# Look-ahead of five pairs in place of eight, inverses in groups of two on two engines, and a later M product, in a chunked scan with two MLPs

## The chip, the cores and the metric

One NeuronCore of a Trainium2 chip runs one launch. Times are microseconds of device time; the span in a profile is the time from the first to the last instruction of one profiled execution. Engines are named as in the profile: PE is TensorE (PEld its weight loads), DVE VectorE, ACT ScalarE, POOL GpSimd, SP SyncE, which only issues DMAs here.

## The reference

For each of 4 x 8 heads a state of 40 x 40 is carried over 768 steps, then two MLPs follow:

```python
for t in range(S):                                   # B, H, S, D = 4, 8, 768, 40
    y[:, :, t] = np.einsum('bhd,bhde->bhe', rt, state)
    Sa = np.einsum('bhde,bhe->bhd', state, at)
    state_decay = state * wt[:, :, None, :] - np.einsum('bhd,bhe->bhde', Sa, bt)
    state = state_decay + np.einsum('bhd,bhe->bhde', vt, kt)
x = y.transpose(0, 2, 1, 3).reshape(3072, 320)
xn = x / rms(x) * rms_g                              # first MLP, d_ff 1536
x = (silu(xn @ w_gate) * (xn @ w_val)) @ w_out
h = x @ w_in                                         # second MLP, d_ff 2048
out = (h - np.tanh(h)) @ w_out2
```

## The kernel before

**Scan.** Time is cut into 12 chunks of 64 steps. A *unit* is one chunk of one batch entry with its eight heads; a *pair* is the same chunk of two entries, so there are 48 units and NP = 24 pairs, and one pass of the main loop, a *period*, deals with one pair. Inside a chunk the recurrence is a triangular system. What it needs is prepared ahead of the loop's current pair, by LOOKP pairs:

- `load_p`, `emit_p` (lines 201 to 231): load a unit, two scans over its decays on VectorE (lines 218 and 222, with a reciprocal at 221), three products on GpSimd (228 to 230). `spill_p` (234) writes the result to HBM, `load_q`, `load_kl` and `load_e` bring the parts back when the pair's turn has come. The first units keep their results in SBUF (`fp`, the pool `first`), later ones use the tile `arena`.
- `emit_m` (236): the product of a pair's units on TensorE (line 247, 32 matmuls), copied by ScalarE and written to HBM as `md` (line 252), by SP's queue where the pool `fp` is used and by ScalarE's queue otherwise.
- `inverse` (254): for a group of pairs (`GROUPS`), the diagonal blocks of M are read back (line 270) and inverted by 31 steps of two instructions on the engine `eng` (lines 276 and 278); the result goes to HBM as `td` (282) and comes back as TT (`load_t`, 347). Group 0 runs on VectorE, all others on GpSimd; groups 0 and 1 have two pairs, the later ones four.

**A period's chain** on TensorE: right side (`emit_rhs`, 397), solve with TT (`emit_u`, 408), product with MX (`emit_w`, 417; VectorE subtracts at 418), solve again (`emit_u2`, 425; `emit_ut`, 472), state (`emit_d`, 437; VectorE at 442 to 448), `emit_z` (482; VectorE 484), `emit_mak` (384; VectorE 387) and `emit_s` (462) for the next pair, `emit_e` (372). The next period finishes the output (`emit_y`, 505 and 507) and normalizes it (`emit_x1`: GpSimd at 514 and 515, VectorE's scaling at 516).

**MLPs.** Between the steps `moe` puts pieces of the first MLP into TensorE's order: an up half (`up`, line 554, 8 matmuls) or a down set (559 to 561, 6 matmuls). It has 12 blocks of 256 tokens with 12 steps of two up halves and one down set each. VectorE joins the halves (576, 578), ScalarE and GpSimd split the result in two (581, 582). Where a call of `moe` finds no piece it issues 8 filler matmuls (`warm`, 288). Until the second block begins, `piece` lets only M_PER pieces through per period, from period M_FIRST on:

```python
if begun[0] < 2 and period[0] < M_FIRST + pieces[0] // M_PER:
    return 0.0
```

The weights come as 64-bit words; a *weight task* (`split_words`, 136 to 151) is one load, ScalarE's absolute value (140), five instructions on VectorE (141 to 146), ScalarE's copy (147) and two instructions on GpSimd (150, 151). The first MLP has 48 tasks: 16 go to tiles that are free from the start, 32 to the pool `w1p`, whose memory is that of `first`. The second MLP's tasks are started by `some2` in the last periods, and go on behind the loop; the last three of its eight chunks use the first MLP's memory.

**Order.** TensorE's instructions stand as the code is written. For the other engines a scheduler sorts them by the priorities that `when`, `later` and `step` set; in the prologue their order is written out too. Each engine then works off its queue in order. `issue_after` only tells the scheduler what must stand ahead.

## Time and profile before

| | us |
|---|---|
| median of 3 runs (lowest, highest) | 1404.84 (1403.24, 1406.26) |
| profiled execution: device time | 1405.97 |
| profiled execution: span | 1403.9 |
| mean granted TensorE clock | 0.937 |

| engine | busy us | share of the span |
|---|---|---|
| PE | 1230.0 | 88% |
| DVE | 689.3 | 49% |
| ACT | 465.2 | 33% |
| POOL | 738.5 | 53% |

First product of a period (line 397), start in us: period 0 at 36.3, 1 at 123.7, 2 at 165.6, 3 at 196.2, 4 at 232.3, 5 at 272.9, 6 at 310.4, 7 at 349.1, 8 at 378.4, 9 at 429.8, 15 at 653.5, 23 at 933.6. The second MLP's first matmul starts at 1032.1. The page's slices are a fortieth of the span each (35.1 us), and a digit is the busy share in tenths. In a table of windows each row gives the stretch, its length, each engine's busy time and number of instructions, the granted clock, the DMA engines' share and GB/s. A row of waits gives the instruction that waited, what released it, the total us, the times, and the longest.

### The profile page before, as it was taken

The numbers are of one execution on the slowest core, as the hardware profiler recorded it, in microseconds if no ns is written. First come the engines' busy times: TensorE is split into PE (matmuls) and PEld (weight loads), VectorE is DVE, ScalarE is ACT, GpSimd is POOL, SyncE is SP. The second block draws the span as 40 slices with busy tenths as digits, with TensorE's granted clock in tenths as the row PEclk, the third lists the DMA queues.
The fourth block names the chain that finished last, engine by engine and source line by source line (L and its number), as shares of the span: only waits on it lengthen the run. The fifth ranks groups of instructions, "written<-read, shape, count | busy, mean of one in ns | idle before, by whom it ended". The sixth has DMA issues, their size and how long they took to land.

```text
span 1403.9 us, 35562 instructions
## 1 busy us (share of the span) xinstructions
PE 1230.0 (88%) x14676; PEld 1133.4 (81%) x14676; DVE 689.3 (49%) x1363; ACT 465.2 (33%) x1077; POOL 738.5 (53%) x1107
## 2 busy tenths in 40 slices
PE   2457677787969999989999999998888999999997
PEld 2346566676869999979999999988876899898997
DVE  6787337777524344434433344445989222222221
ACT  1123123333223333323333343433444333333332
POOL 5488687677916933593329222324666433333332
PEclk9757899888889999989999999999999999999999
DMA  7586566776636455545442333422232001010000
GB/s 192 133 241 163 144 163 165 189 176 148 183 94 148 128 152 144 148 118 147 115 101 70 101 101 91 100 73 75 88 101 80 19 24 31 24 29 19 1 19 20
DMA packets 200212, 149.42 MB, mean 106 GB/s; under 512 B 124626, under 2 KB 174002, under 8 KB 200050
## 3 DMA queue, kind: packets, MB, share of 16 engines
q1 hardware_dynamic: 180463, 133.12, 36.9%
q10 hardware_dynamic: 19587, 14.03, 3.3%
q8 instruction: 115, 1.88, 0.6%
q14 instruction: 47, 0.39, 0.1%
HBM read 105.48 MB, written 41.62 MB: 105 GB/s over the span
## 4 chain that ended last, share of the span: by engine, by line
PE 57%; DVE 10%; POOL 8%; DMA 6%; issue 3%; ACT 1%; SPq 0%; ACTq 0%; POOLq 0%; DVEq 0%
PE ups L554 25%; PE acc L559 6%; PE acc L561 6%; PE acc L560 6%; POOL arena L278 3%; PE turn L482 2%; DMA raw<-in_w_gate_dram 2%; DVE fa L141 2%; POOL tmp L276 2%; DVE fa L143 2%; DVE raw L146 1%; PE solve L425 1%; PE solve L408 1%; DVE fa L142 1%; PE turn L397 1%
## 5 line engine op out<-in xcount | busy, mean ns | idle before, releaser
L554 PE MATMUL ups<-xh,w1c 128*128 128x256 f32 x1440 | 233.5, 293 | 7.8 <-DVE hf L578 6.7
L973 POOL TENSOR_TENSOR hl<-th,hh 128x512 fp32r<-128x512 f32 x96 | 125.4, 1306 | 202.5 <-ACT hh L972 188.1
L582 POOL TENSOR_TENSOR hl<-hf,hh 128x256 fp32r<-128x256 f32 x144 | 109.5, 760 | 222.9 <-ACT hh L581 211.2
L554 PEld LDWEIGHTS ups<-xh,w1c 128*128 128x128 f32 x1440 | 198.3, 194 | 12.6 <-DVE hf L578 8.9
L969 DVE TENSOR_TENSOR th<-ups,th 128x512 f32<-128x512 f32 x96 | 66.3, 690 | 219.2 <-ACT th L968 219.1
L554 PE MATMUL ups<-xl,w1c 128*128 128x256 f32 x864 | 151.8, 285 | 0.0
L576 DVE SCALAR_TENSOR_TENSOR th<-th,ups 128x256 f32<-128x256 f32 x144 | 59.9, 416 | 172.7 <-ACT th L575 172.2
L554 PEld LDWEIGHTS ups<-xl,w1c 128*128 128x128 f32 x864 | 126.0, 194 | 0.0
L581 ACT CAST hh<-hf 128x256 fp32r<-128x256 f32 x144 | 58.4, 405 | 147.2 <-DVE hf L578 138.2
L554 PE MATMUL ups<-yh,w2c 128*128 128x512 f32 x360 | 102.3, 394 | 0.7 <-DVE th L969 0.5
L575 ACT ACTIVATE th<-ups 128x256 f32<-128x256 f32 x144 | 55.0, 382 | 134.8 <-PE ups L554 124.9
L559 PE MATMUL acc<-w1c,hh 128*128 128x320 f32 x288 | 97.1, 337 | 2.9 <-ACT hh L581 2.9
L968 ACT ACTIVATE th<-ups 128x512 f32<-128x512 f32 x96 | 57.1, 595 | 126.0 <-PE ups L554 126.0
L561 PE MATMUL acc<-w1c,hl 128*128 128x320 f32 x288 | 91.5, 318 | 2.1 <-POOL hl L582 2.1
L560 PE MATMUL acc<-w1c,hh 128*128 128x320 f32 x288 | 90.8, 315 | 0.0
L559 PE MATMUL acc<-w2c,hh 128*128 128x320 f32 x288 | 86.8, 312 | 3.6 <-ACT hh L972 3.5
L560 PE MATMUL acc<-w2c,hh 128*128 128x320 f32 x288 | 86.3, 309 | 0.0
L972 ACT CAST hh<-th 128x512 fp32r<-128x512 f32 x96 | 59.6, 620 | 77.3 <-DVE th L969 67.3
L288 PE MATMUL wps<-wz 128*128 128x256 bf16 x516 | 80.7, 312 | 0.0
L276 POOL TENSOR_TENSOR tmp<-arena 128x31 f32<-128x31 f32 (+15 forms) x124 | 65.8, 531 | 21.3 <-DMA arena<-md 14.9
L278 POOL TENSOR_TENSOR arena<-arena,tmp 128x31 f32<-128x31 f32 (+15 forms) x124 | 71.3, 575 | 6.9
L554 PEld LDWEIGHTS ups<-yh,w2c 128*128 128x128 f32 x360 | 65.3, 188 | 11.2 <-DVE th L969 1.3
(153 smaller groups left out, 2887.6 us busy)
## 6 DMA issues: line engine op xcount, KB each, us to landing
RU<-in_vr_dram SPq DMA_DIRECT2D x48, 312.0 KB
arena<-in_abkw_dram SPq DMA_DIRECT2D x32, 418.0 KB
sp<-arena ACTq DMA_DIRECT2D x23, 417.6 KB
kl<-sp SPq DMA_DIRECT2D x22, 416.0 KB
raw<-in_w_out_dram SPq DMA_DIRECT2D x28, 320.0 KB
pl<-in_abkw_dram SPq DMA_DIRECT2D x16, 418.0 KB
sp<-po SPq DMA_DIRECT2D x12, 417.6 KB
xd<-XS SPq DMA_DIRECT2D x24, 192.0 KB
```

Of the source, the lines that this page charges most:

```text
L276: eng.tensor_tensor(out=tv, in0=T[:, :nr, s:s + 1].to_broadcast([128, nr, wd]), in1=M[:, s:s + 1, s + 1:HC].to_broadcast([128, nr, wd]), o ...
L278: lastd[0] = eng.tensor_tensor(out=T[:, :nr, s + 1:HC], in0=T[:, :nr, s + 1:HC], in1=tv, op=ALU.subtract)
L288: PE.matmul(wp[:, 0].rearrange("p (a b) -> p a b", a=2), lhsT=wz[:, 0], rhs=wz.to_broadcast([128, 2, 128]), start=True, stop=True)
L554: PE.matmul(ps, lhsT=l, rhs=r[:, :n], start=i == 0, stop=i == 7)
L559: PE.matmul(acc[t][:, :DM], lhsT=hh[:, c], rhs=oh, start=f == 0, stop=False)
L560: PE.matmul(acc[t][:, :DM], lhsT=hh[:, c], rhs=ol, start=False, stop=False)
L561: PE.matmul(acc[t][:, :DM], lhsT=hl[:, c], rhs=oh, start=False, stop=f == nf - 1)
L576: DVE.scalar_tensor_tensor(out=th, in0=th, scalar=1.0, in1=ps[:, 0], op0=ALU.add, op1=ALU.mult)
L582: POOL.tensor_tensor(out=hl, in0=hf, in1=hh, op=ALU.subtract)
L969: DVE.tensor_tensor(out=th, in0=ps, in1=th, op=ALU.subtract)
L972: ACT.copy(hh, th)
L973: POOL.tensor_tensor(out=hl, in0=th, in1=hh, op=ALU.subtract)
```

## The change

- LOOKP is 5 instead of 8, so each pair's units are scanned five pairs ahead. Loading, scanning and spilling a pair's two units are placed elsewhere in the period (`stage_p` behind `emit_w` and `emit_d`; the new `spill` apart from it, always on SP's queue).
- All groups have two pairs. Even groups are inverted on VectorE, odd ones on GpSimd, group 1 in a tile of its own (`mt`), all others in the same part of `arena`; an inverse is issued in one go (no `held`).
- M is always written by ScalarE's queue. Its product for the pair four ahead stands behind the next period's `emit_u`, where before it stood behind `emit_mak`.
- The pool `first` is closed at period 1 instead of 2, so `w1p` and the first MLP's x tiles begin there; M_PER is 4 instead of 6; `some2` begins in period 21 instead of 18 (by NP - LOOKP + 2). Tiles and counts shrink accordingly.

```diff
@@ constants
-GROUPS = [(0, 2), (2, 4)] + [(g, g + 4) for g in range(4, NP, 4)]
-LOOKP = 8
+GROUPS = [(g, g + 2) for g in range(0, NP, 2)]
+LOOKP = 5
-NPE = 12
+NPE = 8
-M_PER = 6
+M_PER = 4
-AR_P = 2 * HC * HC
+AR_P = HC * HC * 3 // 2
@@ emit_m
-            (SP if pool else ACT).dma_start(out=md_d[gi][p - GROUPS[gi][0], s].rearrange("w q i t -> i (w q) t"), in_=ms[64 * s:64 * s + C])
+            ACT.dma_start(out=md_d[gi][p - GROUPS[gi][0], s].rearrange("w q i t -> i (w q) t"), in_=ms[64 * s:64 * s + C])
@@ prologue
-            i0 = inverse(0, DVE, M0, T0, fp)
+            i0 = inverse(0, DVE, MA, TA, fp)
+            i1 = inverse(1, POOL, mt[:, 0:HC * HC], mt[:, HC * HC:AR_P], fp)
...
+            emit_p(4, fp)
+            emit_p(5, fp)
+            emit_m(2, fp)
...
-            for u in range(6, 8):
-                startp(u)
+            emit_p(6, fp)
+            emit_p(7, fp)
             emit_m(3, fp)
...
-        later(2, run, i1)
+        later(1, emit_p, 8, fp)
+        later(1, emit_p, 9, fp)
+        load_p(10)
+        later(4, run, i1)
@@ stage_p
-                spill_p(u, ACT if u > 24 else SP)
+        def spill(u):
+            if u < NU:
+                spill_p(u, SP)
@@ main loop
-            if p == 2:
+            if p == 1:
...
-                    later(P_LATE, stage_p, 2 * n - 2)
-                else:
-                    later(1, startp, 8)
-                    later(1, startp, 9)
...
                 emit_u(p)
                 if p == 0:
                     load_q(1)
-                    emit_m(4, fp)
-                    later(1, startp, 10)
-                    later(1, startp, 11)
-                step(0.7)
+                elif n - 1 < NP:
+                    spill(2 * n - 1)
+                    emit_m(n - 1)
+                step(1.2)
                 moe(RATE)
                 emit_w(p)
...
+                later(P_LATE, stage_p, 2 * n)
...
                 emit_d(p)
                 load_v(p + 1)
-                if p:
-                    later(P_LATE, stage_p, 2 * n - 1)
-                else:
-                    for u in range(12, 16):
-                        later(1, startp, u)
+                later(P_LATE, stage_p, 2 * n + 1)
+                spill(2 * n)
...
                 if p == 0:
-                    emit_m(6, fp)
-                    emit_m(7, fp)
-                    i2 = inverse(2, POOL, M2, T2, fp)
...
-                    later(10, run, i2)
-                elif n - 1 < NP:
-                    emit_m(n - 1)
+                    emit_m(4, fp)
...
-            if held:
+            if now and p and n - 1 < NP and n == GROUPS[group_of[n - 1]][1]:
+                gi = group_of[n - 1]
                 with tc.issue_after(gate[0].ins), tc.issue_after(gate_pool[0].ins):
-                    later(I_LATE, run, held.pop(0))
-            elif now and p and n - 1 < NP and n == GROUPS[group_of[n - 1]][1]:
-                held.append(inverse(group_of[n - 1], POOL, arena[:, 0:1024], arena[:, 1024:2048]))
-                for _ in range(2):
-                    later(I_LATE, next, held[0])
+                    later(I_LATE, run, inverse(gi, POOL if gi % 2 else DVE, MA, TA))
             elif p >= NP - LOOKP + 2:
                 some2()
```

Line numbers of the changed kernel are one higher up to line 540 or so (218 is 219, 418 is 419, 247 is 248); the old numbers are used below unless it is said otherwise.

What this does to the order is seen at three places. On TensorE, near the end of period 0: `emit_mak` and `emit_s` for pair 1, then M products, among fillers. Before:

```order
L288 MATMUL wps<-wz 128x256
L384 MATMUL turn_160<-Q,po 64x64 x16
L462 MATMUL gapped<-idn,st 40x40 x16
L247 MATMUL turn_161<-po 64x64 x16
L247 MATMUL turn_160<-po 64x64 x16
L288 LDWEIGHTS wz
```

and changed:

```order
L289 MATMUL wps<-wz 128x256
L385 MATMUL turn_170<-Q,po 64x64 x16
L463 MATMUL gapped<-idn,st 40x40 x16
L248 MATMUL turn_171<-po 64x64 x16
L289 LDWEIGHTS wz
```

Pairs 6 and 7 had their product there, now pair 4 has; of pairs 4 and 5, which stood behind the first and the second solve of period 0, pair 5 comes behind period 1's first solve.

On VectorE, between `emit_z` of period 1 and the right side of period 2 (RS, line 399). The scans of `emit_p` carry the name SCALAR_TENSOR_TENSOR with the output sx, po or arena. Before:

```order
L484 TENSOR_TENSOR z<-turn_161,msk 128x512
L387 TENSOR_TENSOR Q<-turn_160,msk 64x2x256 x2
L218 SCALAR_TENSOR_TENSOR sx<-arena,z_175 104x260
L221 RECIPROCAL zr<-sx 104x4
L222 SCALAR_TENSOR_TENSOR arena<-arena,zr 104x260
```

and a part of the same stretch in the changed kernel, where `tmp` and `arena` of lines 277 and 279 are the inverse of group 2, and fa and raw a weight task:

```order
L141 TENSOR_SCALAR fa<-fa 128x320
L277 TENSOR_TENSOR tmp<-arena 128x100
L142 TENSOR_SCALAR fa<-fa 128x320
L279 TENSOR_TENSOR arena<-arena,tmp 128x4x25
L143 SCALAR_TENSOR_TENSOR fa<-raw,fa 128x320
L277 TENSOR_TENSOR tmp<-arena 128x96
L145 TENSOR_SCALAR raw<-fa 128x320
L279 TENSOR_TENSOR arena<-arena,tmp 128x4x24
L146 SCALAR_TENSOR_TENSOR raw<-raw 128x320
```

Weight tasks and an inverse now stand where only scans stood. Over whole periods, the changed order has 9 tasks ahead of period 1's right side, then 12, 14, 9 and 4 in periods 1 to 4 and none until period 22; before it was 16, then 2, 0, 4, 9, 8, 7 and 2 in periods 1 to 7. The MLP's full rate begins in period 11 instead of 8, and behind period 23's right side stand 92 units of 16 up matmuls instead of 70.5 (48 of either are the second MLP's).

On SP's queue, around the write of group 3's inverse, before (td_106, pairs 8 to 11, at period 8's start):

```order
L311 DMA Q<-sp_81 40x2x256
L282 DMA td_106<-arena 128x1024
L317 DMA VS<-in_vn_dram 64x2x160
L326 DMA RU<-in_vr_dram 104x4x192 x2
L518 DMA xd_117<-XS 128x384
L347 DMA TT<-td_106 32x8x32 x4
```

and changed (td_111, pairs 6 and 7, in period 5):

```order
L235 DMA sp_82<-arena 104x1028
L204 DMA arena<-in_abkw_dram 104x1029
L271 DMA arena<-md_100 32x32x32
L283 DMA td_111<-arena 1024x1x32 x2
L322 DMA UV<-in_vn_dram 64x2x320
L271 DMA arena<-md_100 32x32x32 x3
L348 DMA TT<-td_111 32x8x32 x4
```

The write of the inverse now stands ahead of V's load for the next pair and of a part of the next group's read, and the spills of the scanned units (sp_82) share the queue.

More of the change, by code (lines that the diff above doesn't have):

```diff
@@ L653, in wkv_chunks__then__gated_mlp__then__tanh_mlp_kernel @@
         ET = mybir.EngineType
-        M0, M2 = arena[:, 0:1024], arena[:, 0:1024]
-        T0, T1, T2 = arena[:, 1024:1536], arena[:, 1536:2048], arena[:, 1024:2048]
-        M1 = arena[:, AR_P:AR_P + 1024]
-        def startp(u, eng=POOL):
-            emit_p(u, fp, eng)
-            if u >= 2 * KEEP:
-                spill_p(u, SP)
+        MA, TA = arena[:, 0:HC * HC], arena[:, HC * HC:AR_P]
+        mt = fp.tile([128, AR_P], F32, tag="mt", name="mt")
         with tc.manual_schedule(engines={ET.DVE, ET.SP, ET.Activation, ET.Pool}):
@@ L683, in wkv_chunks__then__gated_mlp__then__tanh_mlp_kernel @@
                     emit_m(u // 2, fp)
-            next(i0)
-            for t in (Q, VS, UV, TT, MX):
+            for t in (Q, VS, UV, MX, TT):
                 DVE.memset(t, 0.0)
@@ L690, in wkv_chunks__then__gated_mlp__then__tanh_mlp_kernel @@
             load_v(0)
+            load_r(0)
+            next(i0)
             load_mx(0)
-            load_r(0)
+            for u in range(6, 10):
+                load_p(u, fp)
+            emit_s(0)
+            emit_p(4, fp)
+            emit_p(5, fp)
+            emit_m(2, fp)
             for w in range(2):
                 emit_kb(0, w)
-            emit_s(0)
-            startp(4)
-            for u in range(6, 8):
-                load_p(u, fp)
+            emit_mak(0)
+            load_e(0)
+            emit_rhs(0)
+            next(i1)
             for k in range(HC - 1):
-                if k == 5:
-                    emit_mak(0)
-                    load_e(0)
-                if k == 8:
-                    startp(5)
-                    emit_m(2, fp)
-                if k == 20:
-                    emit_rhs(0)
                 next(i0)
+            spill_p(4, SP)
             run(i0)
@@ L711, in wkv_chunks__then__gated_mlp__then__tanh_mlp_kernel @@
             load_t(0)
+            spill_p(5, SP)
             warm(WARM0)
-            for u in range(6, 8):
-                startp(u)
+            emit_p(6, fp)
+            emit_p(7, fp)
             emit_m(3, fp)
-            i1 = inverse(1, POOL, M1, T1, fp)
             next(i1)
-            next(i1)
-            for u in range(8, 12):
-                load_p(u, fp)
             SP.dma_start(out=gB, in_=rms_g.rearrange("(o n) -> o n", o=1).to_broadcast([128, DM]))
+            spill_p(6, SP)
+            spill_p(7, SP)
         with tc.issue_after(first_w.ins):
@@ L792, in stage_p @@
                     load_p(u + 1)
-                with tc.issue_after((gate[0] or last_t).ins):
+                with tc.issue_after((gate[0] or first_w).ins):
                     emit_p(u)
-                spill_p(u, ACT if u > 24 else SP)
+        def spill(u):
+            if u < NU:
+                spill_p(u, SP)
         todo = []
@@ L828, in wkv_chunks__then__gated_mlp__then__tanh_mlp_kernel @@
                 ma = phA.enter_context(tc.tile_pool(name="ma", bufs=2, side="right", reuse_waits="tile"))
-            if now:
-                if p:
-                    emit_rhs(p)
-                    load_q(p + 1)
-                    later(P_LATE, stage_p, 2 * n - 2)
-                else:
-                    later(1, startp, 8)
-                    later(1, startp, 9)
+            if now and p:
+                emit_rhs(p)
+                load_q(p + 1)
             if p:
@@ L857, in wkv_chunks__then__gated_mlp__then__tanh_mlp_kernel @@
                     emit_kb(p + 1, 0)
+                later(P_LATE, stage_p, 2 * n)
+                if p == 0:
+                    spill(8)
+                    spill(9)
                 step(1.2)
@@ L872, in wkv_chunks__then__gated_mlp__then__tanh_mlp_kernel @@
                 load_v(p + 1)
-                if p:
-                    later(P_LATE, stage_p, 2 * n - 1)
-                else:
-                    for u in range(12, 16):
-                        later(1, startp, u)
+                later(P_LATE, stage_p, 2 * n + 1)
+                spill(2 * n)
                 step(0.8)
-            if p > 1:
+            if p > 0:
                 x2()
@@ L893, in wkv_chunks__then__gated_mlp__then__tanh_mlp_kernel @@
                 if p == 0:
-                    emit_m(6, fp)
-                    emit_m(7, fp)
-                    i2 = inverse(2, POOL, M2, T2, fp)
-                    next(i2)
-                    next(i2)
-                    later(10, run, i2)
-                    last_t = lastd[0]
-                elif n - 1 < NP:
-                    emit_m(n - 1)
+                    emit_m(4, fp)
                 step(1.5)
@@ L907, in wkv_chunks__then__gated_mlp__then__tanh_mlp_kernel @@
                 step(0.4)
-            if p > 1:
+            if p > 0:
                 x2()
```

10 lines of the change are left out of this document (5 added, 5 removed).

## The prediction

> **What bounds the kernel now.** I read the page first (slices, chain), then the waits of TensorE, then a table of windows cut at each period's first product (line 397), then groups and single rows. A period is one pair of scan chunks; its MLP pieces stand between its steps in TensorE's own order.
>
> ```profile
> span 1403.9 us, 35562 instructions
> PE 1230.0 (88%) x14676; PEld 1133.4 (81%) x14676; DVE 689.3 (49%) x1363; ACT 465.2 (33%) x1077; POOL 738.5 (53%) x1107
> ...
> PE   2457677787969999989999999998888999999997
> ...
> DVE  6787337777524344434433344445989222222221
> ```
>
> TensorE is full from slice 13 on, save slices 28 to 31, where VectorE reads 9 and 8. Before slice 13 nothing is full. So three stretches matter: the start, the full periods, and the tail of the first MLP in which the second MLP's weights are prepared. The windows run from period 0's first solve to period 8, then and over periods 8, 15 to 22 and the tail (period 23 to the second MLP):
>
> ```profile
> core 0: us, PE busy (x) PEld busy (x) DVE busy (x) ACT busy (x) POOL busy (x), PEclk, DMA share, GB/s
> 61.40:123.70 62.30, 34.52 (x445) 28.90 (x444) 49.68 (x92) 16.09 (x38) 51.44 (x82) 0.58 0.77 211
> 123.70:165.60 41.90, 25.08 (x421) 21.28 (x420) 20.95 (x39) 8.16 (x19) 28.14 (x63) 0.80 0.57 135
> 165.60:196.20 30.60, 25.05 (x457) 21.91 (x457) 11.44 (x18) 6.54 (x15) 26.55 (x48) 0.89 0.59 152
> ...
> 232.30:272.90 40.60, 28.64 (x480) 25.31 (x479) 33.52 (x72) 15.31 (x40) 27.55 (x35) 0.95 0.71 182
> 272.90:310.40 37.50, 32.25 (x474) 28.46 (x474) 28.54 (x61) 13.51 (x34) 27.22 (x41) 0.79 0.75 180
> 310.40:349.10 38.70, 30.27 (x473) 26.20 (x472) 31.27 (x57) 12.55 (x32) 31.04 (x45) 0.85 0.64 158
> 349.10:378.40 29.30, 29.30 (x475) 27.41 (x474) 19.00 (x32) 9.23 (x22) 26.18 (x40) 0.83 0.64 175
> 378.40:429.80 51.40, 39.31 (x553) 37.80 (x553) 18.58 (x35) 12.97 (x32) 18.96 (x37) 0.87 0.46 116
> ...
> 653.50:933.60 280.10, 276.35 (x4177) 265.63 (x4176) 118.19 (x261) 103.60 (x262) 104.58 (x181) 1.00 0.39 102
> 933.60:1032.10 98.50, 84.96 (x831) 80.15 (x831) 72.31 (x156) 38.64 (x104) 50.03 (x67) 0.95 0.26 77
> ```
>
> Period 8 starts at 378.4. It is the first with MLP at full rate, and it loses some 16 us against the 35.0 of periods 15 to 22 (280.1/8). What TensorE waits for, in the windows from period 0's start to period 2 (first three rows) and in period 8 (last row):
>
> ```profile
> PE turn L247 <- POOL po L228: 15.8, 2, 13.7
> PE turn L247 <- POOL arena L228: 12.5, 2, 10.2
> PE turn L247 <- POOL po L229: 10.8, 2, 7.5
> ...
> PE solve L408 <- DMA TT<-td: 11.3, 1, 11.3
> ```
>
> M's product (line 247) waits on units scanned far ahead, at the head of TensorE's queue; period 8 waits for an inverse that came late.
>
> **The change, part by part.** The sum follows the profiled execution: 1403.9 of span, 1405.97 as device time, thus 2.1 around the span; the median of the runs shown, 1404.84, is 1.1 below it.
>
> *Start to period 1.* Before period 1, VectorE now has 7 scanned units and 9 weight tasks in its order where it had 10 and 16. A unit is two scans and a reciprocal. A task is lines 141 to 146, here from the groups of 232 to 349:
>
> ```profile
> L222 DVE TENSOR_TENSOR_SCAN po<-pl,zr 104x260 f32<-104x260 f32 x8 | 8.2, 1023 | 0.5 <-DMA sp<-po 0.3
> L218 DVE TENSOR_TENSOR_SCAN sx<-pl,z 104x260 f32<-104x260 f32 x8 | 7.6, 947 | 4.1 <-DMA pl<-in_abkw_dram 3.9
> L221 DVE RECIPROCAL zr<-sx 104x4 f32<-104x4 f32 x8 | 1.4, 179 | 0.2
> ...
> L143 DVE SCALAR_TENSOR_TENSOR fa<-raw,fa 128x256 int32<-128x256 int32 (+1 forms) x25 | 15.4, 614 | 0.6
> L142 DVE TENSOR_SCALAR fa<-fa 128x256 int32<-128x256 int32 (+1 forms) x24 | 13.7, 572 | 0.4
> L146 DVE SCALAR_TENSOR_TENSOR raw<-raw 128x256 f32<-128x256 uint32 (+1 forms) x25 | 12.6, 505 | 0.4
> L145 DVE TENSOR_SCALAR raw<-fa 128x256 int32<-128x256 int32 (+1 forms) x25 | 11.6, 463 | 0.4
> L141 DVE TENSOR_SCALAR fa<-fa 128x256 f32<-128x256 f32 (+1 forms) x24 | 10.0, 418 | 20.4 <-ACT fa L140 20.4
> ```
>
> So 3 x 2.15 + 7 x 2.53 = 24 us less. VectorE was busy for 49.7 of the 62.3 us there, and two of the M waits go with the units they waited for. I take all 24: period 1 starts at 99 (nothing saved: 123.7; the M waits gone on top: about 90).
>
> *Periods 1 to 4.* The changed order has 12, 14, 9 and 4 weight tasks there and the whole inverse of group 2, on VectorE. Its price is that of group 0's inverse:
>
> ```profile
> L278 DVE TENSOR_TENSOR arena<-arena,tmph 128x126 f32<-128x126 f32 (+22 forms) x31 | 8.9, 288 | 1.1
> L276 DVE TENSOR_TENSOR tmph<-arena 128x126 f32<-128x126 f32 (+22 forms) x31 | 8.5, 274 | 7.7 <-DMA arena<-md 6.7
> ```
>
> 39 tasks x 2.53 = 98.7; inverse 17.4; the scan's own VectorE work 4 x 11.4 (period 2's busy time, a period without tasks); 3.5 MLP steps, some 3. That is 165. The same sum for periods 4 to 6 of before gives 25 x 2.53 + 3 x 11.4 + 5 = 102 against 116.8 passed, a factor of 1.14 for VectorE's waits. So 188: period 5 starts at 287. (Factor 1: 264; the factor of periods 4 to 6 by busy time, 116.8/93.3 = 1.25: 305.)
>
> *Periods 5 to 10.* No tasks are left, but the MLP stays at 4 pieces a period until period 11, so these are light periods. Nearest are 2 (30.6) and 7 (29.3). In period 7 TensorE never waits, but its first 10 us run at half clock; the same fill of eight matmuls and the same product of 32 later on:
>
> ```profile
> 349.10 1.94 PE L397 MATMUL turn<-VS,Q 128*64 128x40 f32 x32
> ...
> 370.98 1.04 PE L288 MATMUL wps<-wz 128*128 128x256 bf16 x8
> ...
> 375.11 1.13 PE L247 MATMUL turn<-arena 40*64 40x64 f32 x32
> ```
>
> At full clock it would be about 24.3. Ends: 24.3 and 30.6. I take 26.3, nearer the lower, since GpSimd, busy for 26.6 of period 2's 30.6 us, loses half of the inverses: 6 x 26.3 = 158. Period 11 starts at 445.
>
> *Periods 11 to 22.* Twelve full periods stand where fifteen (8 to 22) took 555.2 us. One costs 35.0 by the window; M's product (1.1 us) stands in 9 of 12 instead of 2 of 8, and slightly more MLP work: 35.8. With 5 us for small waits, 434. Period 8's 11.3 us wait goes, as each inverse is issued two periods ahead of its use. The moved M queue behind ScalarE's copy issues the same two DMAs as it did from period 1 on; spills that move from ScalarE's to SP's queue I cost at nothing, since their loads are due a period later; without that cover see the third rival.
>
> *Tail.* By TensorE's order 92 up-units (16 matmuls) now stand behind period 23's start, where it was 70.5, and 22 more sets of six down. Up half and down set:
>
> ```profile
> 541.16 0.86 PE L554 MATMUL ups<-xh,w1c 128*128 128x256 f32 x5
> ...
> 542.22 0.31 PE L559 MATMUL acc<-w1c,hh 128*128 128x320 f32 x1
> ...
> 543.10 0.76 PE L554 MATMUL ups<-xh,w1c 128*128 128x256 f32 x5
> ```
>
> About 0.96 per half, 0.88 per set: 21.5 x 1.93 + 22 x 0.88 = 60.5. The old tail had some 18 us of idle TensorE, 98.5 less 80 of work (22.5 x 1.93, 23 x 0.88, 17 of scan), while VectorE was busy for 72. The new work fills 10 of it: 98.5 + 60.5 - 10 = 149. Weights prepared late come later still, since two periods' tasks move into the tail; their cover is the longer tail.
>
> *The rest* (1032.1 to the end) stays 371.8. Sum: 445 + 434 + 149 + 372 = 1400 of span, 1402 as device time, 1401 against the median: **1400 us**.
>
> **Rivals.**
> 1. *Light periods as short as what TensorE issues*, 24.3: 12 us less, 1388. For it: period 7 from 361 on. Against: every other early period waited somewhere.
> 2. *Slower: light periods stay at 30.6.* VectorE's queue holds x's scaling (line 516), which needs GpSimd, ahead of the solve's subtraction (line 418); period 2:
>
> ```profile
> 178.46 0.87 DVE L516 SCALAR_TENSOR_TENSOR XS<-XA,ss,gB 128x320 f32<-128x320 f32 x1 [6.83 <-POOL ss L515]
> 179.25 0.47 DVE L418 TENSOR_TENSOR RS<-RS,turn 128x320 f32<-128x320 f32 x1
> ```
>
> VectorE stood still for 6.83 us, and the solve with it, because GpSimd was at an inverse. Now an inverse on VectorE itself falls into periods 5 and 6 and another into 9 and 10, whose 62 instructions lie among these two, and GpSimd works at group 3's until period 5. Price 6 x (30.6 - 26.3) = 26, thus 1426. It decides from a mean of some 27.0 on: 1401 + 6 x 0.65 is 1405.
> 3. *The late transposed inverse again.* In SP's changed order the write of group 3's inverse (td_111) stands ahead of the loads of V, T and the next keys. If GpSimd ends it after period 5, period 6 pays what period 8 paid: 11.3 us, and some 5 at a lower clock (0.87 there). 1416. Against: 39 tasks are through by then, and GpSimd has about 20 instruction pairs left.
> 4. *VectorE and GpSimd in each other's way.* The same inverse instruction (128x110), beside GpSimd's three products of a unit and alone:
>
> ```profile
> 34.68 0.63 DVE L276 TENSOR_TENSOR tmph<-arena 128x110 f32<-128x110 f32 x1
> ...
> 44.23 0.27 DVE L276 TENSOR_TENSOR tmph<-arena 128x110 f32<-128x110 f32 x1
> ```
>
> 0.36 us more each. My 17.4 for group 2's inverse comes from a stretch where GpSimd was mostly idle; in the heavy stretch of period 0 it was busy for 51.4 of 62.3. All 62 instructions beside a busy GpSimd: 62 x 0.36 x 0.83 = 18 more, 1419. Half of that is in the factor 1.14 already, which comes from periods with the same neighbours. The Trainium skill has this as a rule (GPSIMD Engine Reference, section "Key points": GpSimd shares its SBUF interfaces with VectorE, and VectorE instructions with two SBUF inputs contend for them); by that rule moving inverses to VectorE speeds up neither engine as much as their separate times say, and the trace agrees with 0.63 against 0.27 us.
>
> Another rule bears on the light periods. The page shows granted clocks of 0.79 to 0.85 in three of the early periods above, and 1.00 from period 15 on. The Trainium skill (TensorE: Matmul & The Clock Gate, "Part 1: The HAM clock gate") says that the array falls to half clock after an idle window of some 3.4 us and needs as much steady work to leave it. By that rule a light period is 24.3 us unless a single wait is longer than such a window, so it speaks for the first rival or for the second, and for little between them.
>
> **How the numbers follow.** Chances: the forecast (1390 to 1411) 0.38; rival 1 0.20; rival 2 0.25; rival 3 0.09; rival 4 0.08. The changed kernel can be told from the old one from about 0.2% on, 2.8 us. The forecast's own range straddles this: I give it 0.23 faster, 0.10 same, 0.05 slower, as it is centred 4 us below. Rival 1 is faster. Rival 2 spans 1403 to 1430: 0.04 same, 0.21 slower. Rivals 3 and 4 are slower, with 0.02 same between them. Faster 0.43, same 0.16, slower 0.41. The two open prices carry the range: VectorE's factor (1 to 1.25, -23 to +17) and the light period (24.3 to 30.6, -12 to +26). Both low would give 1366, both high 1443; with one of them at its end and the other halfway it is 1372 to 1432, which I take for 8 in 10.
>
> **What the profile would show.** Right: period 1's first product (line 398) near 99, period 5's near 287, period 11's near 445; no wait of TensorE for M's product above 5 us; periods 11 to 22 near 36 each; the second MLP starting near 1028. Wrong in the start: weight tasks of line 146 later than period 5, or VectorE waiting for line 140 longer than before. Wrong in the light periods: a mean above 27 with VectorE idle before line 517 or 419. Wrong in the tail: the second MLP's first block longer than 66.4, as its last three chunks are prepared only when the first MLP's memory comes free. What would upset the whole is a wait in the full periods, since each of twelve would pay it: at 1 us each that is 12 us, three times the gain.

## Result and profile after

The changed kernel takes 1447.2 us (median of 4 runs, 1442.62 to 1450.65) against 1405.55 of the old one in the same comparison: a ratio of 1.0276, 95% interval 1.0211 to 1.0342. The prediction was 1400 with a range to 1432: its sign is wrong, and the time lies outside the range. The profiled execution took 1448.0 as device time, 1446.2 as span. Most lines carry a number one higher than before (397 is now 398, 418 is 419, 516 is 517).

From the page of the changed kernel, the busy times and the forty slices (36.2 us each) of TensorE and VectorE:

```profile
span 1446.2 us, 36421 instructions
...
PE 1252.2 (87%) x14884; PEld 1151.9 (80%) x14884; DVE 773.6 (53%) x1673; ACT 468.2 (32%) x1077; POOL 687.2 (48%) x1127
...
PE   3466268798797999998999999988998999999997
...
DVE  4859878747346534843483333599539422222221
```

TensorE was busy for 22 us more than before (1252.2 against 1230.0) and VectorE for 84 more. So the 42 us cannot all be new waiting; about half is work, or the same work at a lower clock. The table of windows cut where the prediction's sum was cut: period 0, periods 1 to 4, 5 to 10, 11 to 22, the tail, the second MLP.

```profile
33.90:108.50 74.60, 41.97 (x480) 34.29 (x481) 54.44 (x132) 11.62 (x27) 44.09 (x75) 0.68 0.56 142
108.50:294.10 185.60, 118.40 (x1821) 102.81 (x1820) 154.85 (x341) 59.71 (x147) 127.02 (x202) 0.74 0.65 163
294.10:476.20 182.10, 154.23 (x2795) 139.74 (x2794) 97.45 (x243) 42.70 (x100) 75.04 (x174) 0.90 0.67 155
476.20:912.90 436.70, 424.61 (x6363) 408.92 (x6362) 216.77 (x500) 149.87 (x374) 192.35 (x407) 0.98 0.49 121
912.90:1074.40 161.50, 146.65 (x1319) 139.36 (x1319) 110.42 (x233) 61.79 (x165) 77.41 (x103) 1.00 0.24 70
1074.40:1446.20 371.80, 355.97 (x1982) 318.10 (x1980) 122.58 (x193) 136.53 (x254) 151.05 (x128) 1.00 0.12 33
```

| stretch | forecast | measured | off by |
|---|---|---|---|
| to period 1 | 99 | 108.5 | +9.5 |
| periods 1 to 4 | 188 | 185.6 | -2.4 |
| periods 5 to 10 | 158 | 182.1 | +24.1 |
| periods 11 to 22 | 434 | 436.7 | +2.7 |
| tail | 149 | 161.5 | +12.5 |
| second MLP | 372 | 371.8 | -0.2 |

Against the old kernel, which began period 11 at 504.8, the new one is 28.6 us ahead at that point; it loses 7.9 in the full periods and 63.0 in the tail (161.5 for 98.5). The MLP work that the pace of 4 held back was to be paid by a start some 60 us shorter, and the start gave half of that.

The waits of TensorE over the whole span:

```profile
PE turn L248 <- POOL po L230: 38.6, 8, 16.0
PE solve L426 <- DVE RS L419: 36.7, 14, 9.5
PE turn L533 <- DMA xin<-xd: 28.9, 1, 28.9
PE ups L555 <- DVE hf L579: 13.6, 18, 1.8
```

The second row is the solve waiting for VectorE's subtraction; the old kernel had 19.5 us of it. The third was not foreseen at all. x's first transposes now stand in period 1: the change runs `x2()` under `if p > 0:` in place of `if p > 1:`, two lines that the diff ahead of the prediction does not show. There they stand at the head of TensorE's queue before x is loaded. SP's queue shows why it comes late:

```profile
120.91 0.42 SPq L519 DMA_DIRECT2D xd<-XS  x1
...
155.06 1.28 SPq L283 DMA_DIRECT2D td<-mt  x2
158.69 1.81 SPq L348 DMA_DIRECT2D TT<-td  x4
160.60 0.40 SPq L527 DMA_DIRECT2D xin<-xd  x1
```

x is written at 120.91, but its load stands behind the write of group 1's inverse (`mt`) and the loads of TT from it. GpSimd works at that inverse from 81 to 155 us, among weight tasks and scanned units. The six light periods, 5 to 10:

```profile
294.10:319.70 25.60, 23.91 (x469) 21.83 (x468) 11.77 (x22) 7.63 (x18) 16.43 (x40) 1.00 0.71 170
319.70:353.80 34.10, 27.44 (x467) 24.29 (x467) 26.01 (x81) 6.63 (x16) 7.83 (x17) 0.85 0.64 147
353.80:377.70 23.90, 23.89 (x468) 21.75 (x468) 10.31 (x19) 6.96 (x16) 7.44 (x15) 1.00 0.81 180
377.70:412.90 35.20, 25.66 (x469) 23.50 (x468) 11.73 (x21) 7.62 (x18) 25.70 (x62) 0.85 0.62 139
412.90:444.80 31.90, 23.88 (x467) 21.70 (x467) 11.29 (x23) 6.90 (x16) 11.51 (x29) 0.93 0.74 171
444.80:476.20 31.40, 29.46 (x468) 26.67 (x468) 26.34 (x78) 6.96 (x16) 6.13 (x12) 0.80 0.54 133
```

Two of them run as the first rival said: 25.6 and 23.9 us at a clock of 1.00. The other four take 31 to 35. In three of these an engine holds an inverse: VectorE is busy for 26 us in periods 6 and 10, GpSimd for 25.7 in period 8; the inverse of period 10 begins at the end of period 9. Of the 38.7 us above six times 23.9, 27.9 are time in which TensorE was not busy (182.1 less 154.2), and 10.8 are the same instructions at a lower clock (154.2 less 143.4). TensorE's two largest rows of waits in these six periods are the one for the subtraction, and one for which the profile shows nothing that was waited for ("issue"):

```profile
PE solve L426 <- DVE RS L419: 17.0, 5, 9.5
PE turn L398 <- issue: 7.8, 2, 7.5
```

The longest of the first row, 9.5 us in period 8, in the timelines of GpSimd, VectorE and TensorE:

```profile
383.21 0.24 POOL L277 TENSOR_TENSOR tmp<-arena 128x31 f32<-128x31 f32 x1 [7.20 <-DMA arena<-md]
...
391.74 0.19 POOL L515 TENSOR_SCALAR ss<-ss 128x1 f32<-128x1 f32 x1
...
392.39 0.56 POOL L516 TENSOR_TENSOR ss<-ss,cm 128x1 f32<-128x1 f32 x1
...
392.98 0.67 DVE L517 SCALAR_TENSOR_TENSOR XS<-XA,ss,gB 128x320 f32<-128x320 f32 x1 [9.83 <-POOL ss L516]
...
398.80 1.50 PE L426 MATMUL solve<-RS,TT 64*64 64x40 f32 x23 [9.54 <-DVE RS L419]
```

The inverse's first instruction waits 7.20 us in GpSimd's queue for its read of M. Behind it and 20 more of its kind stand the two instructions of x's reciprocal root (515, 516); VectorE's scaling waits 9.83 us for them; behind that, and behind the two scans of a unit, stands the subtraction, and TensorE waits 9.54 us. The longest of the second row, at the end of period 9, in those of VectorE and TensorE:

```profile
442.77 0.19 DVE L277 TENSOR_TENSOR tmp<-arena 128x31 f32<-128x31 f32 x1 [7.70 <-DMA arena<-md]
...
443.27 1.39 DVE L388 TENSOR_TENSOR Q<-turn,msk 64x512 f32<-64x512 f32 x2
444.76 1.51 PE L398 MATMUL turn<-VS,Q 128*64 128x40 f32 x24 [7.46 <-issue]
```

Here an inverse on VectorE waits 7.70 us for its read, and the mask of Q (388), which the next period's first product reads, stands behind it. So both long waits have one form: an inverse stands in an engine's queue ahead of a small instruction that TensorE needs.

### The profile page after: what moved, and what is told of

Same layout as the page of the kernel before. It is cut to its first block, busy times and chain, and to the rows that moved or that the text cites. A ratio compares the mean times of both kernels' runs of the same rounds, so it can differ in the third digit from the quotient of the medians.

```text
span 1446.2 us, 36421 instructions
## 1 busy us (share of the span) xinstructions
PE 1252.2 (87%) x14884; PEld 1151.9 (80%) x14884; DVE 773.6 (53%) x1673; ACT 468.2 (32%) x1077; POOL 687.2 (48%) x1127
## 4 chain that ended last, share of the span: by engine, by line
PE 54%; DVE 20%; POOL 8%; DMA 8%; issue 7%; SPq 2%; ACT 1%; ACTq 0%; POOLq 0%; DVEq 0%
PE ups L555 21%; PE acc L560 5%; PE acc L562 5%; PE acc L561 5%; PE wps L289 3%; DVE fa L143 3%; PE turn L483 2%; DVE fa L141 2%; DVE arena L279 2%; DVE raw L146 2%; DMA raw<-in_w_val_dram 2%; PE solve L426 2%; DVE fa L142 2%; PE turn L473 2%; DVE tmp L277 1%
## 5 line engine op out<-in xcount | busy, mean ns | idle before, releaser
L555 PE MATMUL ups<-xh,w1c 128*128 128x256 f32 x1440 | 233.4, 293 | 13.7 <-DVE hf L579 13.6
L577 DVE SCALAR_TENSOR_TENSOR th<-th,ups 128x256 f32<-128x256 f32 x144 | 60.0, 417 | 154.2 <-ACT th L576 154.0
L289 PE MATMUL wps<-wz 128*128 128x256 bf16 x724 | 107.3, 300 | 0.0
L560 PE MATMUL acc<-w1c,hh 128*128 128x320 f32 x288 | 94.0, 327 | 0.9 <-ACT xo L597 0.7
L561 PE MATMUL acc<-w1c,hh 128*128 128x320 f32 x288 | 89.4, 310 | 0.0
L289 PEld LDWEIGHTS <-wz 128*128 128x128 bf16 x724 | 74.9, 107 | 14.2
L277 POOL TENSOR_TENSOR tmp<-arena 128x56 f32<-128x56 f32 (+22 forms) x155 | 58.5, 378 | 35.9 <-DMA arena<-md 22.5
```

What stands on the lines that cost most here:

```text
L277: eng.tensor_tensor(out=tv, in0=T[:, :nr, s:s + 1].to_broadcast([128, nr, wd]), in1=M[:, s:s + 1, s + 1:HC].to_broadcast([128, nr, wd]), o ...
L289: PE.matmul(wp[:, 0].rearrange("p (a b) -> p a b", a=2), lhsT=wz[:, 0], rhs=wz.to_broadcast([128, 2, 128]), start=True, stop=True)
L555: PE.matmul(ps, lhsT=l, rhs=r[:, :n], start=i == 0, stop=i == 7)
L560: PE.matmul(acc[t][:, :DM], lhsT=hh[:, c], rhs=oh, start=f == 0, stop=False)
L561: PE.matmul(acc[t][:, :DM], lhsT=hh[:, c], rhs=ol, start=False, stop=False)
L577: DVE.scalar_tensor_tensor(out=th, in0=th, scalar=1.0, in1=ps[:, 0], op0=ALU.add, op1=ALU.mult)
```

## Experiments

**The pace alone, in both directions.** One number in the changed kernel, twice, and the reverse in the old one.

```diff
 e1, e2: the changed kernel        e3: the old kernel
-M_PER = 4                         -M_PER = 6
+M_PER = 6      (e2: 12)           +M_PER = 4
```

> The changed kernel with the first MLP block let in at 6 pieces a period, as in the old kernel, in place of 4. Theory (the pace): the changed kernel's 42 us over the old one are mostly first-MLP work held back into the tail. Full periods should begin at period 8 or 9 in place of 11; each period made full costs some 6 us more (36.4 against 30.4) and takes 4.7 steps x 2.81 = 13 us off the tail, so 3 periods give about 20 us: 1427 us, with the tail from period 23 to the second MLP near 120 in place of 161. Rival (the short look-ahead and the inverses by turns are what costs, the pace little): 1440 or more.

> The changed kernel with 12 pieces a period for the first block, so that it is through in periods 3 to 5, about when the weight preparation ends (284 us in the changed kernel). Theory (the pace): full periods from period 6 on, five more than now, 5 x 7 = 35 us, less some waits for weights in periods 3 and 4: 1405 to 1418 us, level with the old kernel or a little behind. Rival (VectorE and GpSimd are the bound of the early periods): they grow by what the MLP adds on these engines, and the time stays at 1435 or more.

> The old kernel with one number changed: 4 pieces a period for the first MLP block in place of 6. Theory (the pace): its periods from 8 to 10 become light, each some 5 us shorter, and 13 us of MLP work from each go into the tail: 1405 + 24 = about 1429 us. Rival (the old kernel's tail has room, 18 us of idle TensorE, and takes the work in): 1405 to 1412.

e1 took 1418.74, ratio 1.0076 (1.0053 to 1.0098); e2 1427.07, 1.0137 (1.0094 to 1.0181); e3 1436.02, 1.0204 (1.0178 to 1.0231). So the pace of 4 costs 28 us in either kernel, more than the 20 and 24 I had put on it. The rest of the change costs 0.7% at either pace: 1.0276 against 1.0204 at 4, and 1.0076 against 1 at 6. Windows of e1 for periods 8 to 22 and the tail, and of e3 for the tail:

```profile
381.90:938.60 556.70, 534.50 (x8003) 513.78 (x8002) 282.51 (x659) 187.00 (x466) 249.56 (x532) 0.98 0.51 124
938.60:1046.10 107.50, 86.72 (x832) 81.19 (x832) 87.81 (x181) 43.01 (x115) 61.39 (x79) 0.92 0.28 84
```

```profile
904.10:1057.90 153.80, 144.50 (x1319) 139.28 (x1319) 93.00 (x203) 57.52 (x153) 67.62 (x91) 1.00 0.21 62
```

With the old pace the tail's 1319 matmuls are 832 again. The rival of e3, a tail with room, did not come: the tail took in only 5 of the 60 us. e2 came in neither of its ranges and was no better than e1: from period 9 on its MLP does 12 steps in two periods, as many as two pairs of x feed, and its tail is 107.2, as in e1; what it adds lies in the early periods, where periods 5 to 7 take 111.3 us against 85.7 in e1.

**x's transposes from period 2 on.**

```diff
-            if p > 0:
+            if p > 1:
                 x2()          # both places
```

> The changed kernel with x's first load and transposes only from period 2 on, as in the old kernel (in the changed one the first stands in period 1, where TensorE waited 28.9 us for the load of x). Theory: VectorE was busy for 48.6 of that period's 57.1 us, so the wait covers what VectorE needs anyhow; 5 to 10 us are saved there and all of it arrives at the end: 1437 to 1442. Rival (the transposes' wait is the lost time itself): 20 to 28 us less, 1420 to 1427. Second rival: the period's end is set by other work, no change, 1447.

1436.36, ratio 1.0201 (1.0175 to 1.0228); the span is 8.8 us shorter than the changed kernel's. The intervals of the two kernels overlap, so the gain is not shown by the times alone. Periods 1 and 2 of this kernel,

```profile
110.10:141.70 31.60, 24.19 (x421) 20.98 (x421) 23.23 (x47) 9.54 (x24) 24.03 (x45) 0.82 0.72 172
141.70:206.10 64.40, 34.34 (x457) 29.39 (x457) 61.45 (x160) 19.43 (x48) 39.25 (x57) 0.63 0.59 151
```

Period 1 is 25.5 us shorter, period 2 is 7.7 longer, with VectorE busy for 61.5 of its 64.4 us. At period 5 this kernel is 12.5 us ahead, at the end 8.8. The size is the first theory's, within 1 us of its range, but not all that is saved arrives, and its reason is only half of it. In period 2 the solve now waits 15.5 us for TT, where the changed kernel has no such wait: it is group 1's inverse again, written at 157.87 here. So the 28.9 us covered a wait for the same inverse as well as VectorE's work.

**The read of M ahead of the inverse.**

```diff
                 spill(2 * n)
+                if p and n - 1 < NP and n == GROUPS[group_of[n - 1]][1]:
+                    held.append(inverse(...))
+                    for _ in range(2): next(held[0])   # zero fill, reads
...
-                    later(I_LATE, run, inverse(...))
+                    later(I_LATE, run, held.pop(0))
```

> The changed kernel with each inverse begun in two steps: its zero fill and its four reads of M are issued in the middle of the period, behind the state update, and its 62 instructions at the period's end as before (M is written early in the same period). Theory (an in-order queue held up): the inverse's first instruction waits for its read, 34 us in all over the kernel, and holds back x's scaling and the solve behind it; with the read ahead of need these waits vanish, the light periods 5 to 10 fall from 30.4 to about 27 on average and the 40 us periods (12, 14, 16, 18) to 36: 20 to 30 us in all, 1417 to 1427. Rival (the inverses' own work on VectorE and GpSimd makes these periods long, not the wait for the read): 1440 to 1450, with other waits in the same periods.

1441.92, ratio 1.0211 (1.0189 to 1.0233): the theory's 20 to 30 us did not come, and the time lies in the rival's range. The span is 5.9 us shorter, and periods 5 to 10 take 177.6 in place of 182.1. In period 8 the reads, issued from 369.3 on, held up the inverse's start until 380.3, 1.1 us into the period (383.2 before, 5.5 into it), and the queue behind went on as it did:

```profile
380.33 0.24 POOL L277 TENSOR_TENSOR tmp<-arena 128x31 f32<-128x31 f32 x1 [12.75 <-DMA arena<-md]
...
390.10 0.19 POOL L515 TENSOR_SCALAR ss<-ss 128x1 f32<-128x1 f32 x1
```

Between the two stand 9.8 us with 22 of the inverse's instructions, busy for 7.4. So in period 8 the larger part lies with the place of the 62 instructions. The read still came late, though 4.4 us earlier in the period than before, so its own price stays open.

**All inverses from the third on by GpSimd.**

```diff
-inverse(gi, POOL if gi % 2 else DVE, MA, TA)
+inverse(gi, POOL, MA, TA)
```

> The changed kernel with all inverses from the third on by GpSimd, none by VectorE. Theory (queue held up by the read): the stand moves from VectorE's queue to GpSimd's, where x's scaling stands behind it too, and a pair of instructions takes a third longer there: 1445 to 1460. Rival (the work by turns on VectorE, beside GpSimd on the same memory, is what costs): VectorE loses 45 us of work in periods 2 to 20 and the light periods shorten: 1425 to 1440.

1452.91, ratio 1.0303 (1.0279 to 1.0327), inside the first theory's range; the interval overlaps that of the changed kernel, so it is no faster rather than shown slower. Periods 1 to 4 gain 12.6 us (173.0), as VectorE loses work in its fullest stretch, and periods 5 to 10 lose 9.2 (191.3). The turns between the engines are not what costs in the light periods.

**The 62 instructions behind the next period's subtraction.** The zero fill and the reads stay where they were.

```diff
-        DVE.tensor_tensor(out=RS, in0=RS, in1=tv, op=ALU.subtract)
+        gate_w[0] = DVE.tensor_tensor(out=RS, in0=RS, in1=tv, op=ALU.subtract)
...
                 emit_w(p)
+                if held:
+                    with tc.issue_after(gate_w[0].ins):
+                        later(I_LATE, run, held.pop(0))
...
+                held.append(inverse(...))
-                    later(I_LATE, run, inverse(...))
+                    for _ in range(2): later(I_LATE, next, held[0])
```

> The changed kernel with each inverse's 62 instructions put behind the solve's subtraction of the next period (line 419 of the changed kernel) on their engine; zero fill and reads of M stay where they are. Theory (what the look at the early-read kernel left: it is not only the read, the 62 instructions themselves stand in the queue ahead of x's scaling and the solve's subtraction): TensorE's waits for line 419, 37 us in all, fall to under 12; periods 5 to 10 fall from 30.4 to 27 on average, the 40 us periods to 36; 25 to 40 us less, 1407 to 1422. Rival (the wait only moves to the state update and the masks of the same period, line 443, 485 and 388, which then stand behind the inverse): 1437 to 1450.

1419.95, ratio 1.0092 (1.0073 to 1.0110): 27 us, inside the expected 25 to 40. The windows of periods 5 to 10 and 11 to 22, and TensorE's waits in the first of them:

```profile
291.50:454.20 162.70, 149.82 (x2793) 135.55 (x2793) 89.42 (x210) 42.66 (x100) 79.85 (x184) 0.96 0.73 172
454.20:885.80 431.60, 421.80 (x6360) 405.88 (x6360) 225.96 (x534) 149.46 (x374) 191.96 (x407) 0.99 0.50 123
```

```profile
PE solve L426 <- DVE RS L419: 8.7, 5, 2.7
PE solve L409 <- DMA TT<-td: 1.9, 2, 1.2
```

Practically the same matmuls (2793 for 2795) take 162.7 us in place of 182.1, a mean of 27.1; the clock is 0.96 for 0.90. The waits for line 419 in these periods fall from 17.0 to 8.7 us, and the one of 7.5 ahead of line 398 is gone. VectorE's scaling in period 8 waits 2.41 us for GpSimd, not 9.83. Since the 62 instructions took the wait for their read along with them, the run prices both together. The full periods gain 5.1, the four of 40 us only in part (36.1, 35.2, 41.4, 36.1): the expectation put 16 us on them. The waits for line 419 over the whole span went from 36.7 to 27.5, not under 12; the early ones, in periods that weight tasks fill, stay.

**Weight preparation of the second MLP from period 21 on, in the old kernel.**

```diff
-            elif p >= NP - LOOKP + 2:
+            elif p >= NP - 3:
```

> The old kernel with the preparation of the second MLP's weights between its periods begun at period 21 in place of 18, where a look-ahead of 5 puts it. Theory (the tail's growth beside the pace): six weight tasks more stand in the tail, where VectorE is busy for 72 of 98 us; at 2.5 us each that is 15 more, of which 9 are seen (the changed kernel at the old pace has a tail of 107.5 in place of 98.5): 1405 + 9 = about 1414 us. Rival (the tail of the changed kernel is longer for its late x alone): no change, 1405.

1417.74 against 1409.8 of the old kernel in the same comparison, ratio 1.0046 (1.0031 to 1.0061). The tail has 23 weight tasks in place of 19 and takes 107.2 us in place of 98.5, as expected, with VectorE busy for 87.7 (72.3 before):

```profile
931.00:1038.20 107.20, 85.34 (x831) 79.82 (x831) 87.66 (x180) 43.19 (x115) 61.49 (x79) 0.93 0.28 85
```

This is a price of the shorter look-ahead that the list of constants hides: `some2` may start only when the last inverse has left the arena, and the code ties that to LOOKP.

**M written by SP's queue at the start, as before.**

```diff
-            ACT.dma_start(out=md_d[gi]...)
+            (SP if pool else ACT).dma_start(out=md_d[gi]...)
```

> The changed kernel with the start's products M written by SP's queue, as in the old kernel, in place of ScalarE's. Theory (the writer costs nothing): within 3 us of the changed kernel, 1444 to 1450, period 1 at 108 as before. Rival (on ScalarE's queue the writes stand behind its copies and the start waits for them, which is the missing 9.5 us there): period 1 begins 5 to 10 us sooner, 1438 to 1442.

1429.51, ratio 1.0148 (1.0129 to 1.0166): 17.7 us, more than either theory. ScalarE and its queue in the changed kernel, then in this one:

```profile
17.60 1.49 ACTq L253 DMA_DIRECT2D md<-ms  x2
19.18 0.58 ACT L250 COPY ms<-turn 128x512 f32<-128x512 f32 x1 [1.22 <-DVE sx L219]
19.80 3.88 ACTq L253 DMA_DIRECT2D md<-ms  x2
23.78 1.43 ACT L315 COPY Q<-po 64x256 f32<-64x256 f32 x4 [4.01 <-DMA arena<-in_abkw_dram]
...
27.24 3.22 ACTq L253 DMA_DIRECT2D md<-ms  x2
30.50 0.75 ACT L366 COPY kb<-turn 128x320 f32<-128x320 f32 x2 [4.45 <-DMA md<-ms]
```

```profile
18.25 1.43 ACT L315 COPY Q<-po 64x256 f32<-64x256 f32 x4
25.34 0.59 ACT L250 COPY ms<-turn 128x512 f32<-128x512 f32 x1 [5.66 <-PE turn L248]
26.17 0.43 ACT L366 COPY kb<-turn 128x320 f32<-128x320 f32 x1 [0.24 <-PE turn L364]
```

Issuing two writes holds ScalarE's queue for 3.88 and 3.22 us, and the copies of Q and kb stand behind it. The Trainium skill (DMA: Bandwidth & Descriptors, "Rules for kernel authors") says that spreading DMAs over engines saves nothing but the sequencer's issue time; here that time is the cost, since ScalarE's sequencer had work waiting. So the first product starts at 33.9 in the changed kernel and at 29.7 here. That is 4.2 us; the rest comes in period 2 (34.6 us for 56.7) and goes in part again in periods 5 and 6 (70.1 for 59.7). In period 2 the scheduler had put 8 weight tasks in place of 14 into VectorE's queue, and group 1's inverse was written 6 us sooner (149.0 for 155.1). Three runs ask whether the writer or the order of the tasks made the rest.

**The weight tasks alone.**

```diff
-                    prep1(range(EARLY1, KF1 // 2), w1p)     # in period 1
+            if p in (1, 3, 4, 5):
+                with tc.issue_after((last_t if p == 1 else gate[0]).ins):
+                    prep1([max(p, 2)], w1p)
```

> The changed kernel with the weight preparation of the first MLP's chunks 3, 4 and 5 begun in periods 3, 4 and 5 in place of 1, so that 5 weight tasks in place of 14 stand in VectorE's queue in period 2, and 7 each in periods 4 and 5; M is written by ScalarE's queue as in the changed kernel. Theory (the order of the weight tasks is what the other writer changed): period 2 falls from 57 to about 35 us, periods 4 to 6 grow a little, the whole 10 to 20 us less: 1427 to 1437. Rival (the writer's queue itself costs it): period 2 shortens, but the time is lost again in periods 3 to 6, where the same tasks then stand: 1442 to 1450.

1446.35, ratio 1.0264 (1.0241 to 1.0287): the rival. Period 2 fell to 38.6, and periods 4 to 6 took 114.8 in place of 94.1. At period 11 both stand at 476. Here the tasks' place is worth nothing by itself: VectorE does them in period 2 or in periods 4 to 6, and the solve waits there.

**Combinations.** e7 takes e1, e4, e5 and the second MLP's weights from period 20; e10 adds e9's place of the 62 instructions (reads as in e5); e13 is e10 with e12's spread, e14 is e13 with SP's queue, e15 is e10 with SP's queue, e16 is the changed kernel with e1, e9, SP's queue and the weights from period 20.

> The changed kernel with 6 pieces a period, x's first transposes from period 2 on, the inverse's reads issued in mid-period, and the second MLP's first weights from period 20 on in place of 21. If the three causes add (28.5 for the pace and 11 for the transposes as measured, some 20 for the reads, 3 for the weights in the tail), 1447 - 62 = 1385 us, ahead of the old kernel. Rival (they overlap, as all lie on the same early periods): 1400 to 1410, level with it.

> The combined kernel (6 pieces, x's transposes from period 2 on, early reads, second MLP's weights from period 20) with the 62 instructions behind the next period's subtraction as well. Theory: its periods 12, 14, 16, 18 of 40 us shorten to 36 or 37, and its light ones by 2 each: 1404.7 - 20 = 1385. Rival (the wait only moves): 1400 to 1408.

> The second combined kernel with the weight tasks spread the same way (11 in place of 13 stand in period 2, 6 in place of 2 in period 6). Theory: little is left to gain, as x's late transposes thin period 1 already: 1390 to 1395 against 1395.1. Rival (the spread is worth the same as alone): 1380.

> The same with M written by SP's queue at the start. Theory (order only): within 4 us of the kernel before it, 1387 to 1397. Rival (the writer's queue itself): 10 to 17 us less, 1375 to 1385.

> The second combined kernel (1395.1 us) with M written by SP's queue at the start and nothing else. Theory (4 us are the writer's, the rest the order of the weight tasks, which here is 14 in period 2 against 13): 1388 to 1396. Rival (the writer is worth 17 us anywhere): 1374 to 1381.

> The changed kernel with four edits: 6 pieces a period, the inverse's 62 instructions behind the next period's subtraction, M written by SP's queue at the start, the second MLP's weights from period 20; x's first transposes stay in period 1. In VectorE's queue 7 weight tasks stand in period 2. If the single gains add: 1447 - 28 - 27 - 18 - 3 = 1371. Rival (they overlap, as with the other combinations, which gave 0.7 to 0.8 of the sum): 1385 to 1395.

| kernel | us | ratio to the old kernel, interval | of what was expected |
|---|---|---|---|
| e7 | 1404.69 | 0.9962 (0.9944 to 0.9980) | the rival: the gains overlap |
| e10 | 1395.10 | 0.9914 (0.9899 to 0.9928) | between theory and rival |
| e13 | 1397.88 | 0.9935 (0.9919 to 0.9951) | 3 us above the theory |
| e14 | 1397.70 | 0.9926 (0.9909 to 0.9943) | the theory, 1 us above its range |
| e15 | 1394.34 | 0.9890 (0.9856 to 0.9924) | the theory |
| e16 | 1396.73 | 0.9914 (0.9883 to 0.9946) | the rival, 2 us above its range |

SP's queue changes nothing beside e10 or e13 (0.8 and 0.2 us), though the first product is some 4 us sooner there too (29.8 and 30.1 for 34.0 and 33.9). The traces say where the lead goes: all four kernels wait for TT in period 2 (10.9 us at the longest in e10, 13.2 in e15, 11.4 in e13, 13.1 in e14), and SP's queue does not bring group 1's inverse forward there (149.2 for 149.7, 152.3 for 149.8), as it did in e11. So the other 13 us of e11 hang on what else stands in the early queues; which step is worth them stays open, as the weight tasks' place alone is not it. e16 fell short of the sum by 26: its period 2 is short as in e11 (35.2 us), but 12 weight tasks stand in its period 4, which takes 54.7. In e10, whose profiled execution took 1388.91, 6 us under its median, periods 1 to 4, 5 to 7, 8 to 22 and the tail:

```profile
108.20:275.00 166.80, 118.11 (x1833) 103.42 (x1832) 144.30 (x327) 57.80 (x145) 123.32 (x188) 0.79 0.69 173
275.00:366.40 91.40, 83.64 (x1418) 77.54 (x1417) 57.20 (x140) 24.66 (x59) 47.59 (x100) 0.89 0.69 167
366.40:907.00 540.60, 529.97 (x8003) 509.96 (x8002) 284.74 (x669) 187.41 (x470) 247.71 (x522) 0.99 0.52 128
907.00:1013.10 106.10, 86.59 (x832) 82.00 (x832) 83.89 (x177) 41.54 (x112) 57.78 (x75) 0.91 0.27 83
```

Fifteen full periods take 540.6 in place of the old kernel's 555.2, with the same MLP steps, and period 8 begins 12 us sooner than its 378.4. The 14.6 us are about what the old kernel lost to the late inverse in period 8 alone (some 16). So a kernel with the shorter look-ahead can be 0.9% ahead, with the pace as it was, the inverse behind the solve, and three smaller edits. No run asks whether the old kernel would win as much by mending its period 8 or by the same place of its inverses.

## Why the prediction was wrong

- *Periods 5 to 10: the step that failed.* I put 26.3 a period between 24.3 and 30.6, "nearer the lower", because GpSimd loses half of the inverses. 30.4 came, 24.1 us in all. It is the second rival's number and, in period 8, its place: x's scaling ahead of the subtraction, with an inverse in the queue. At the end of period 9 the same thing happens ahead of another instruction, the mask of Q, which no rival named. e9 shows the cause: with the 62 instructions behind the subtraction the mean is 27.1. The sign of being wrong that the prediction gave, a mean above 27 with VectorE idle before line 517, came true. The error was to weigh the engine's busy time, when the wait is set by what stands ahead of one instruction in a queue, which the order of the changed kernel showed. A mean between two ends described no period: of six, two were at 24 to 26, four at 31 to 35.
- *Start, +9.5.* I took all 24 us of VectorE's lost work and costed M's writer at nothing, calling the queue unchanged "from period 1 on"; the start was where it had changed. e11 measures 4.2 us at the first product, 3.3 of them left at period 1. In period 0 M's product still waits 19.9 us for GpSimd's units (16.0 the longest), so "no wait of TensorE for M's product above 5 us" was wrong.
- *Periods 1 to 4, right by luck.* 185.6 came for 188, but the sum had no wait for x and none for group 1's inverse, and did not ask in what order SP's queue would load x. Without x's wait (e4) the stretch takes 171.5, so the sum of VectorE's work with its factor of 1.14 was too high by about what the missing wait cost. Its prices were right: the inverse of group 2 took 19.2 us of VectorE's time for 17.4.
- *Periods 11 to 22, right in the sum*: 436.7 for 434. The make-up was another: of periods 12 to 18 every second one took 39 to 41 us, with an inverse in it, and the others at most 35.9.
- *Tail, +12.5.* TensorE's work there is 146.7 where I had counted 140.5, and it idles for 15 us, not 8. The old tail's idle time was misread: its row has 84.96 us of busy TensorE in 98.5, so 13.5 us, not 18. I named the moved weight tasks and covered them with the longer tail; e8 prices them at 9 us. At the pace of 4 it is 7.7: the old kernel's tail at that pace takes 153.8 (e3), the changed one 161.5. TensorE waits 18 times (13.6 us) for VectorE's second join of the halves (line 579).
- *The rivals.* Rival 3 did not come where it was looked for: no wait for TT in periods 5 to 10 is among the waits of the changed kernel. A late inverse, group 1's, did hold TensorE earlier: at the end of period 1 here, by x's load behind its write, and in period 2 of e4 and e10 by TT itself. Rival 4 did not come: it put 18 us more on the inverse of group 2 than 17.4, and that took 19.2 in all. The clock followed the waits: of periods 5 to 10, the four with a wait above 3 us, or right after one, had 0.80 to 0.93, the two with none above 1.7 us had 1.00; with none above 2.7 us (e9) it was 0.96 over all six. This agrees in the main with the rule of the Trainium skill quoted in the prediction (TensorE: Matmul & The Clock Gate, "Part 1: The HAM clock gate"); the longest wait of period 6, at 0.85, was 3.2 us, a little under the window of some 3.4 us quoted there.
- *The form of the sum.* The forecast of -4 was the difference of 60 us won at the start and some 56 lost behind it. An error of a fifteenth in either decides the sign. The range was taken from two open prices and left out that the tail and the start had errors of their own, both upward. Even both open prices at their high ends gave only 1443. One reading of the slices was loose: TensorE reads 9 in slice 11 and 8 in slice 18, which carries nothing in the sum.

## What to carry to other kernels

When a change trades work held back against a shorter start, price the two separately: run or reason the throttle (here one number, 28 us in both kernels) without the rest. Before a long run of instructions moves to another engine, read in that engine's queue what stands behind its first and last instruction; the chain of small instructions that the bottleneck waits for must stand ahead of it; where it did not, an earlier read won 5 us, and the right place 27. When a wait is put down to a load, look in the issuing queue for what held that load back: here x's load stood behind the write of an inverse, and taking its wait away uncovered a wait for the same inverse. A constant that looks like one knob (the look-ahead) may also set when unrelated work begins.

## What was not expected of the hardware

Two small DMA issues held ScalarE's queue for 3.88 and 3.22 us (1.49 the first time), longer than any of its copies (1.43 for four). SP needed 2.72 for four such writes in e11, where the copies did not stand behind it. No run shows why the same issue takes 1.49 us once and 3.88 another time. A lead won early can vanish: in e12 18 us of period 2 came back as 21 in periods 4 to 6, and in e14 and e15 4 us at the first product came back as a longer wait for TT in period 2.
